# Loading and using the k-v-gate columns later in the first projection block, with six warming products in place of nine

## The chip, the cores and the metric

The kernel runs on one core of one Trainium2 chip. Time is device time in microseconds of one launch. The core has TensorE (PE, with its weight loads PEld), VectorE (DVE), ScalarE (ACT), GpSimd (POOL) and SyncE (SP); here SP issues all transfers of the kernel, and DMA engines carry them out.

## The reference

Two layers on the same tokens x (2048 x 640), mixed by a gate. The first is a Fourier mixing, real part of a transform over the hidden and the sequence axis, written as products with cosine and sine matrices. The second is attention of 32 heads of 20 with one shared key and value:

```
g = sigmoid((x * gate_w).sum(-1, keepdims=True))
a = Cr @ (x @ Wr.T) - Ci @ (x @ Wi.T)
q = heads(x @ wq);  k = x @ wk;  v = x @ wv
b = merge(softmax(q k^T / sqrt(20)) v) @ wo
out = g * a + (1 - g) * b
```

## The kernel before

Every fp32 operand of a product is kept as two parts: a high part rounded by ACT into the fp32r type, and a low part, the rest, computed by DVE. A product of two operands is then three products of parts: high by high, high by low, low by high (mm3, lines 122 to 124). In the names, wqh and wql are the parts of q's weights, xh and xl those of the transposed tokens, qh and ql those of q.

**The first stage**, where the change is, computes q, k, v and the gate's logits. The tokens are cut into four blocks of 512 (n = 0 to 3) and the hidden axis into five chunks of 128 (c = 0 to 4). q has five output groups of 128 rows (m = 0 to 4). k, v and the gate's column of weights stand side by side as 41 columns in one input, wkvg; its tile kvg is split into high columns 0 to 40 and low columns 64 to 104 of the tile kvgs. kv_mm (line 395) sends two products per chunk: one of xh with all 105 columns, one of xl with the high 41. In the last chunk their order is reversed.

Block 0 goes chunk by chunk, since the weights arrive chunk by chunk: load_x1 and move issue the loads (SP), split_x1 and split make the parts (ACT the high one, line 378 and 117; DVE the low one, line 379 and 118), then follow the chunk's k-v products and fifteen q products into six open PSUM banks. Blocks 1 to 3 go group by group.

Before the first data come, PE multiplies the identity by itself (line 106). These are the warming products; each is recorded as two pieces.

When a block's k-v sum is done, kv_out (line 402) evicts it: kvl (ACT, 408), kvT (DVE, 409), kh (ACT, 410), kl (DVE, 411), and six copies of kh and kl into the tile ks, which holds the keys for the score products. q_out (line 386) does the same for a q group: qh (ACT, 390), ql (DVE, 391), and two stores to the DRAM tensors qh_d and ql_d. load_qs0 (line 156) reads a first head pair back from there into the tile qs. The score products a (line 251), which search for the largest score of each query, are strewn among the q products of blocks 1 to 3, four at a time.

**Order.** PE, ACT, DVE and POOL execute in the order in which the program is written; so does SP's queue, except that loads are moved ahead to where their buffer is free. qh and ql have three buffers each, so the fourth qh of a block waits until the store of the first is done. Banks are taken by turns: line 350 for block 0, line 468 for the others, with four banks F1, V, S0 and F0. In block 1 the k-v sum takes F1, the transposed k-v of block 0 takes V, q groups 0 and 1 take S0 and F0, and q group 2 takes F1 again, once kv_out has emptied it.

The later stages are the Fourier products, attention and the output projection, interlaced on PE by hand-written orders. The change doesn't touch them.

## Time and profile before

| what | value |
|---|---|
| median of 3 runs | 1725.58 us (1724.9 to 1726.78) |
| profiled execution: span | 1723.7 us |
| profiled execution: time outside the span | not recorded; the median is 1.9 us above the span |
| PE busy | 1706.9 us, 99% of the span |
| DVE, ACT, POOL busy | 1379.9, 1251.9, 1103.8 us |
| granted TensorE clock, mean | 0.999 |
| block 0's first k-v product, block 1's first | at 5.95 and 26.47 us |

A row of the timeline gives the start and the duration in us, the engine, the line, the operation with what it writes and reads, and in brackets how long the engine had been idle before and what ended that. Starts of consecutive products are closer together than one product's duration, since PE overlaps them. A row SPq is SP issuing a transfer, not the transfer.

### The profile page before, as it was taken

The numbers are of one execution on the slowest core, as the hardware profiler recorded it, in microseconds if no ns is written. First come the engines' busy times: TensorE is split into PE (matmuls) and PEld (weight loads), VectorE is DVE, ScalarE is ACT, GpSimd is POOL, SyncE is SP. The second block draws the span as 40 slices with busy tenths as digits, with TensorE's granted clock in tenths as the row PEclk, the third lists the DMA queues.
The fourth block names the chain that finished last, engine by engine and source line by source line (L and its number), as shares of the span: only waits on it lengthen the run. The fifth ranks groups of instructions, "written<-read, shape, count | busy, mean of one in ns | idle before, by whom it ended". The sixth has DMA issues, their size and how long they took to land.

```text
span 1723.7 us, 43339 instructions
## 1 busy us (share of the span) xinstructions
PE 1706.9 (99%) x16754; PEld 1235.3 (72%) x16754; DVE 1379.9 (80%) x2294; ACT 1251.9 (73%) x2547; POOL 1103.8 (64%) x923
## 2 busy tenths in 40 slices
PE   9999999999999999999999999999999999999997
PEld 6686677777777777777777777777777777777665
DVE  4788888888888888888888888888888888888823
ACT  4247788888777677777777777777777767678896
POOL 0154556333356658758777888888887765547786
PEclk9999999999999999999999999999999999999999
DMA  8651223222275556546666666655555533143332
GB/s 251 190 157 58 72 79 106 79 71 72 65 232 170 172 164 198 170 157 201 220 214 218 226 233 227 205 186 184 177 179 165 159 113 114 52 128 110 108 94 95
DMA packets 180346, 261.46 MB, mean 152 GB/s; under 512 B 35568, under 2 KB 134128, under 8 KB 180140
## 3 DMA queue, kind: packets, MB, share of 16 engines
q1 hardware_dynamic: 180140, 258.70, 47.4%
q8 instruction: 132, 2.16, 0.5%
q14 instruction: 74, 0.61, 0.1%
HBM read 184.42 MB, written 76.99 MB: 152 GB/s over the span
## 4 chain that ended last, share of the span: by engine, by line
PE 96%; DMA 1%; ACT 1%; DVE 1%; SPq 1%; issue 1%; POOL 0%; DVEq 0%; ACTq 0%
PE av L983 27%; PE y_p L791 21%; PE b L971 18%; PE a L251 15%; PE ab L791 7%; PE oo L791 3%; PE q L122 1%; PE q L124 1%; PE q L123 1%; SPq L114 1%; ACT pt L979 1%; DMA qh_d<-qh 1%; PE kv L400 0%; DMA wraw<-in_wq_dram 0%; DVE pt L1028 0%
## 5 line engine op out<-in xcount | busy, mean ns | idle before, releaser
L258 DVE TENSOR_REDUCE mx<-a 128x1 f32<-128x512 f32 x2048 | 1304.4, 686 | 243.7 <-PE a L251 206.0
L979 ACT ACTIVATE pt<-b 128x512 f32<-128x512 f32 x2048 | 1058.5, 624 | 342.7 <-PE a L251 279.2
L971 PE MATMUL b<-qs,ks 62*128 62x512 f32 x2048 | 756.9, 408 | 2.2 <-ACT pt L979 1.4
L251 PE MATMUL a<-ks,qs 60*128 60x512 f32 x2048 | 704.2, 407 | 3.6 <-DMA qs<-ql_d 2.3
L791 PE MATMUL y_p<-tb,ch 64*128 64x320 f32 x3584 | 618.7, 307 | 0.0
L791 PEld LDWEIGHTS y_p<-tb,ch 64*128 64x128 f32 x3584 | 504.5, 186 | 2.9
L983 PE MATMUL av<-pt,vsb 128*32 128x512 f32 x4096 | 484.9, 597 | 0.0
L971 PEld LDWEIGHTS b<-qs,ks 62*128 62x128 f32 x2048 | 346.1, 184 | 186.4 <-DVE mx L258 124.2
L791 PE MATMUL y_p<-tb,cl 64*128 64x320 f32 x1792 | 455.5, 306 | 0.0
L251 PEld LDWEIGHTS a<-ks,qs 60*128 60x128 f32 x2048 | 345.2, 185 | 18.0 <-issue 4.7
L791 PEld LDWEIGHTS y_p<-tb,cl 64*128 64x128 f32 x1792 | 297.2, 185 | 2.8
L983 PEld LDWEIGHTS av<-pt,vsb 128*32 128x32 f32 x4096 | 111.4, 109 | 239.5 <-issue 229.6
L551 POOL TENSOR_TENSOR cl<-craw,ch 128x1024 fp32r<-128x1024 f32 x112 | 268.3, 2395 | 9.0
L833 POOL TENSOR_TENSOR yt<-yt,yu 128x320 f32<-128x320 f32 x86 | 75.8, 881 | 292.6 <-ACT yu L828 242.5
L833 POOL TENSOR_TENSOR abt<-abt,abu 128x320 f32<-128x320 f32 x64 | 55.7, 871 | 196.0 <-ACT abu L828 183.4
L545 POOL TENSOR_TENSOR craw<-craw 128x1024 f32<-128x1024 f32 x64 | 153.3, 2396 | 0.0
L550 POOL CAST ch<-craw 128x1024 fp32r<-128x1024 f32 x112 | 116.3, 1038 | 6.3 <-PE ab L791 2.2
L791 PE MATMUL oo<-wo,osp 64*128 64x320 f32 x816 | 91.6, 306 | 0.0
L791 PEld LDWEIGHTS oo<-wo,osp 64*128 64x128 f32 x816 | 86.7, 185 | 1.6
L577 POOL TENSOR_TENSOR tb<-braw,tb 128x320 fp32r<-128x320 f32 x80 | 69.7, 877 | 0.0
L791 PE MATMUL ab<-wbh,xh 64*128 64x320 f32 x256 | 59.4, 307 | 0.0
L791 PE MATMUL ab<-wbh,xl 64*128 64x320 f32 x256 | 59.3, 305 | 0.0
(138 smaller groups left out, 1604.0 us busy)
## 6 DMA issues: line engine op xcount, KB each, us to landing
craw<-in_cre_dram SPq DMA_DIRECT2D x80, 512.0 KB
craw<-in_cim_dram SPq DMA_DIRECT2D x64, 512.0 KB
s_d<-craw SPq DMA_DIRECT2D x32, 512.0 KB
craw<-s_d SPq DMA_DIRECT2D x32, 512.0 KB
braw<-b_d SPq DMA_DIRECT2D x80, 160.0 KB
xraw<-in_xT_dram SPq DMA_DIRECT2D x32, 320.0 KB
b_d<-abt SPq DMA_DIRECT2D x64, 160.0 KB
t_d<-braw SPq DMA_DIRECT2D x64, 160.0 KB
```

The source lines that it names most:

```text
L114: nc.sync.dma_start(words(dst), words(src))
L251: nc.tensor.matmul(ps, qs[v][b : b + 60, qb * P : (qb + 1) * P], ks[b : b + 60, c * ROW : (c + 1) * ROW], start=True, stop=True,)
L258: nc.vector.tensor_reduce(mx[v][:, hh, qb, c : c + 1], ps, axis=AX.X, op=ALU.max)
L545: nc.gpsimd.tensor_tensor(x, raw[0], x, op=how)
L550: nc.gpsimd.tensor_copy(h, x)
L551: nc.gpsimd.tensor_tensor(l, x, h.bitcast(F32), op=ALU.subtract)
L577: nc.gpsimd.tensor_tensor(t[:, 1], raw, t[:, 0].bitcast(F32), op=ALU.subtract)
L791: nc.tensor.matmul(ps, w, x, start=start, stop=stop)
L833: nc.gpsimd.tensor_tensor(t0, t0, t1, op=ALU.add)
L971: nc.tensor.matmul(ps, ks[b : b + 62, kc * P : (kc + 1) * P], qs[NPAIR * (qc // 2) + p][b : b + 62, (qc % 2) * ROW : (qc % 2 + 1) * ROW], ...
L979: nc.scalar.activation(t, ps, AF.Exp, scale=SCALE)
L983: nc.tensor.matmul(ps[32 * g : 32 * g + 32, :], vsb[:, kc, :], t, start=first, stop=last)
```

## The change

Four things are changed, all in the first stage.

- The load of kvg is issued behind the second chunk of q's weights, not ahead of the first, and it is split into kvgs after the second chunk's splits.
- Block 0's k-v products of a chunk are sent one chunk later: those of chunk c - 1 go behind the first two q groups of chunk c. The last chunk's go behind its third q group.
- The first chunk's q products go by terms: five high by high, five with xl, five with wql, each over the five groups.
- Six warming products are sent in place of nine.

```
--- before.py
+++ after.py
@@ -102,7 +102,7 @@
     omg = const.tile([P, NT], F32, name="omg")
 
     warm = bank("S4", "warm")
-    for _ in range(9):
+    for _ in range(6):
         nc.tensor.matmul(warm[:, :P], ident, ident, start=True, stop=True)
 
     nc.scalar.activation(gate, ident[:, :NT], AF.Exp)
@@ -437,7 +437,6 @@
             nc.vector.tensor_scalar(omg, gate, -1.0, 1.0, op0=ALU.mult, op1=ALU.add)
 
         load_x1(0, 0)
-        move(kvg, wkvg.rearrange("(c p) n -> p c n", p=P))
         pkv = rot("kv_0")
         pq = [rot(f"q_0_{m}") for m in range(KC)]
         for c in range(KC):
@@ -445,16 +444,27 @@
                 load_x1(0, c)
             raw = raw_tile([P, D], "wraw") if c in (2, 3) else w1.tile([P, D], F32, name="wraw", bufs=2)
             move(raw, wq_v[:, c])
-            if c == 0:
+            if c == 1:
+                move(kvg, wkvg.rearrange("(c p) n -> p c n", p=P))
+            split_x1(0, c)
+            split(raw, wqh[:, c], wql[:, c])
+            if c == 1:
                 nc.vector.tensor_copy(kvgs[:, :, :41], kvg)
                 nc.vector.tensor_tensor(
                     kvgs[:, :, 64:105], kvg, kvgs[:, :, :41].bitcast(F32), op=ALU.subtract
                 )
-            split_x1(0, c)
-            split(raw, wqh[:, c], wql[:, c])
-            kv_mm(pkv, 0, c)
+            if c == 0:
+                xh, xl = xsp[0]
+                for k, (w, x) in enumerate(((wqh, xh), (wqh, xl), (wql, xh))):
+                    for m in range(KC):
+                        nc.tensor.matmul(pq[m], w[:, 0, m * P : (m + 1) * P], x[:, 0], start=(k == 0), stop=False)
+                continue
             for m in range(KC):
                 q_mm(pq[m], 0, m, c)
+                if m == 1:
+                    kv_mm(pkv, 0, c - 1)
+                elif m == 2 and c == KC - 1:
+                    kv_mm(pkv, 0, c)
         for c in range(KC):
             load_x1(1, c)
         for c in range(KC):
```

In the changed kernel the lines from 438 on lie up to ten lines further down; the first chunk's q products are line 460 there, and the k-v-gate split is lines 452 and 453.

## The prediction

> **What bounds the kernel now.** I read the page first, then the waits of PE, then the timeline of the first 55 us, then the chain there. From the page, the span, PE's row and the chain that ended last:

> ```profile
> span 1723.7 us, 43339 instructions
> ...
> PE 1706.9 (99%) x16754; PEld 1235.3 (72%) x16754; DVE 1379.9 (80%) x2294; ACT 1251.9 (73%) x2547; POOL 1103.8 (64%) x923
> ...
> PE 96%; DMA 1%; ACT 1%; DVE 1%; SPq 1%; issue 1%; POOL 0%; DVEq 0%; ACTq 0%
> ```

> PE has work for 99% of the span, and the change neither removes nor adds a real product (only three warming ones go). So all that can move the time is when PE begins, at which clock, and how long it waits. The longest waits of PE over the whole run (total us, times, longest us):

> ```profile
> PE a L251 <- DMA qs<-ql_d: 2.3, 3, 1.0
> PE b L971 <- ACT pt L979: 1.4, 2, 0.7
> PE warm L106 <- POOL ident masks.py:199: 1.3, 1, 1.3
> PE o L122 <- DVE acc L774: 1.3, 1, 1.3
> PE a L251 <- DVE mx L258: 1.3, 1, 1.3
> PE q L122 <- DVE kvT L409: 0.9, 1, 0.9
> PE kv L400 <- DVE kvgs L450: 0.7, 1, 0.7
> ```

> The first, sixth and seventh row lie in the first 54 us, where the change is. The others come after that, or before the change, and follow PE's own pace. The beginning, from the timeline (start, us, engine, line):

> ```profile
> 1.17 0.42 SPq L114 DMA_DIRECT2D kvg<-in_wkvg_dram  x1
> 1.34 3.88 PE L106 MATMUL warm<-ident 128*128 128x128 f32 x18 [1.34 <-POOL ident masks.py:199]
> 1.63 0.52 SPq L114 DMA_DIRECT2D wraw<-in_wq_dram  x1
> 4.30 0.63 ACT L378 ACTIVATE xh<-xr 128x512 fp32r<-128x512 f32 x1 [2.08 <-DMA xr<-in_xT_dram]
> 5.03 0.37 DVE L449 CAST kvgs<-kvg 128x205 fp32r<-128x205 f32 x1 [5.03 <-DMA kvg<-in_wkvg_dram]
> 5.82 0.74 ACT L117 ACTIVATE wqh<-wraw 128x640 fp32r<-128x640 f32 x1 [0.89 <-DMA wraw<-in_wq_dram]
> 5.95 0.45 PE L400 MATMUL kv<-xh,kvgs 128*105 128x512 f32 x1 [0.73 <-DVE kvgs L450]
> 6.59 0.82 DVE L118 TENSOR_TENSOR wql<-wraw,wqh 128x640 fp32r<-128x640 f32 x1 [0.19 <-ACT wqh L117]
> 7.47 0.50 PE L124 MATMUL q<-xh,wql 128*128 128x512 f32 x1
> 7.81 0.39 PE L122 MATMUL q<-xh,wqh 128*128 128x512 f32 x1
> 8.89 0.83 DVE L118 TENSOR_TENSOR wql<-wraw,wqh 128x640 fp32r<-128x640 f32 x1 [0.18 <-ACT wqh L117]
> ```

> Two k-v products start at 5.95, one waits, two q products follow, and PE stands until wql is there (6.59 + 0.82 = 7.41). From 7.81 on it runs without a gap. The other end of this block, and what hangs on its k-v sum:

> ```profile
> 22.74 0.39 PE L400 MATMUL kv<-xh,kvgs 128*105 128x512 f32 x1
> 23.16 0.59 ACT L408 ACTIVATE kvl<-kv 41x512 f32<-41x512 f32 x1 [4.97 <-PE kv L400]
> 25.20 0.90 SPq L114 DMA_DIRECT2D ks<-kh  x1
> 26.47 0.40 PE L400 MATMUL kv<-xh,kvgs 128*105 128x512 f32 x1
> 30.06 0.42 SPq L114 DMA_DIRECT2D qh_d<-qh  x1
> 34.86 0.60 ACT L390 ACTIVATE qh<-q 128x512 fp32r<-128x512 f32 x1 [1.60 <-DMA qh_d<-qh]
> 36.55 0.67 DVE L409 TENSOR_TENSOR kvT<-kv,kvl 41x512 f32<-41x512 f32 x1
> 37.37 0.47 PE L122 MATMUL q<-xh,wqh 128*128 128x512 f32 x1 [0.87 <-DVE kvT L409]
> 42.09 1.19 PE L251 MATMUL a<-ks,qs 60*128 60x512 f32 x4 [0.98 <-DMA qs<-ql_d]
> 51.92 0.46 PE L251 MATMUL a<-ks,qs 60*128 60x512 f32 x1 [0.58 <-DMA qs<-ql_d]
> 53.11 0.70 PE L251 MATMUL a<-ks,qs 60*128 60x512 f32 x3 [0.73 <-DMA qs<-ql_d]
> ```

> The reader should see one chain here. The last k-v product of the block (22.74) ends it for ACT (23.16). kvl, kvT and kh follow, and then SP, which had stood idle, issues the first ks copy at 25.20. SP is now the narrow place: six ks copies, ten q stores behind them, six qs loads behind those, all in order on one queue. ACT's fifth qh waits for a store to free its buffer (34.86), kvl and kvT of the next block queue behind it, and PE waits at 37.37 for the bank that this kvT empties. The score products at 42.09, 51.92 and 53.11 wait for qs loads on the same queue. The chain view has the store itself, which competes with nothing but this chain:

> ```profile
> 31.05 3.71 DMA qh_d<-qh
> ```

> After 53.11 PE waits for nothing of SP's. So where PE stands at 53.11 is set by the moment at which the block's k-v sum is ready, with no play between, and not by the moment at which PE begins.

> **The change, part by part.** SP's queue at the start, of before and then of now (xr0 is the tokens' chunk, wraw the chunk of q's weights, kvg the k-v-gate columns):

> ```order
> L114 DMA xr0_144<-in_xT_dram 128x512
> L114 DMA kvg_137<-in_wkvg_dram 128x5x41
> L114 DMA wraw_153<-in_wq_dram 128x640
> L114 DMA xr0_180<-in_xT_dram 128x512
> L114 DMA wraw_182<-in_wq_dram 128x640
> ```

> ```order
> L114 DMA xr0_141<-in_xT_dram 128x512
> L114 DMA wraw_149<-in_wq_dram 128x640
> L114 DMA xr0_172<-in_xT_dram 128x512
> L114 DMA wraw_174<-in_wq_dram 128x640
> L114 DMA kvg_134<-in_wkvg_dram 128x5x41
> ```

> Four loads move up one place and kvg goes behind them. The first wraw is issued 1.63 - 1.17 = 0.46 us sooner, and kvg's bytes no longer go ahead of it: it landed 5.82 - 5.03 = 0.79 after kvg. I take 0.6, between these, so it lands at 5.22. ACT is free then (4.30 + 0.63 = 4.93), wqh is ready at 5.22 + 0.74 = 5.96, and PE starts 0.06 later as it did after wql (7.41, 7.47): first q product at **6.02**. Bounds: 5.73 when ACT never waits for the load, 6.62 when the load gains nothing.

> With five high products first, then five with xl, then five with wql, nothing waits in that chunk: xl is ready by 4.93 + 0.69 + a little, five products before its use, and wql at 5.96 + 0.03 + 0.82 = 6.81, ten before its use. The spacing of products comes from before: 80 products from 7.81 to 26.47 are 0.2333 us each; the first of a stretch takes 0.34 (7.47 to 7.81). Product 15, the first of chunk 1, starts at 6.02 + 0.34 + 14 x 0.2333 = 9.63, its first use of wql at 10.1; that wql was done at 8.89 + 0.83 = 9.72 even by before's loads. The two kvgs operations (0.37 each) go behind it on DVE, done by 10.5, and their first product is number 21, at 11.0. Queued behind them is chunk 2's xl and wql (1.5 us), used at 13.6: covered. Were the cover gone, each would cost its 0.74.

> PE's end of the block and the next block's first product, before (of the 15 q products behind the k-v pair only nine are shown) and now:

> ```order
> L124 MATMUL q_4_152<-xh,wql 128x512
> L400 MATMUL kv_147<-xl,kvgs 41x512
> L400 MATMUL kv_147<-xh,kvgs 105x512
> L122 MATMUL q_0_148<-xh,wqh 128x512
> L123 MATMUL q_0_148<-xl,wqh 128x512
> L124 MATMUL q_0_148<-xh,wql 128x512
> L122 MATMUL q_1_149<-xh,wqh 128x512
> L123 MATMUL q_1_149<-xl,wqh 128x512
> L124 MATMUL q_1_149<-xh,wql 128x512
> L122 MATMUL q_2_150<-xh,wqh 128x512
> L123 MATMUL q_2_150<-xl,wqh 128x512
> L124 MATMUL q_2_150<-xh,wql 128x512
> ```

> ```order
> L122 MATMUL q_2_146<-xh,wqh 128x512
> L123 MATMUL q_2_146<-xl,wqh 128x512
> L124 MATMUL q_2_146<-xh,wql 128x512
> L400 MATMUL kv_143<-xl,kvgs 41x512
> L400 MATMUL kv_143<-xh,kvgs 105x512
> L122 MATMUL q_3_147<-xh,wqh 128x512
> L123 MATMUL q_3_147<-xl,wqh 128x512
> L124 MATMUL q_3_147<-xh,wql 128x512
> L122 MATMUL q_4_148<-xh,wqh 128x512
> L123 MATMUL q_4_148<-xl,wqh 128x512
> L124 MATMUL q_4_148<-xh,wql 128x512
> L400 MATMUL kv_357<-xh,kvgs 105x512
> ```

> The last k-v product had fifteen products behind it and now has six: it was number 70 of the block's 85 and is number 79. It starts at 6.02 + 0.34 + 77 x 0.2333 = 24.33, where it started at 22.74: **1.6 us later**. The block itself ends sooner: 6.02 + 0.34 + 84 x 0.2333 = 25.96 against 26.47, **0.5 us sooner**. By the chain above the first number reaches PE whole, at 37.37 (now 38.95), and the second is spent waiting there: PE arrives earlier and waits some 3 us instead of 0.87. The later waits of 0.98, 0.58 and 0.73 stay as they are, since both sides moved by 1.6. In between, the evictions of q run 1.6 later as well, and PE needs the first of their banks only at 28.7, when ql0 is out at about 28.0.

> The three warming products: 18 pieces took 3.88, so twelve take 2.6 and end at 3.9. PE was idle from 5.22 anyway, so no time is won. What they may cost is the clock. All pieces of the warming, least, median and longest ns, and the last weight loads:

> ```profile
> L106 PEld LDWEIGHTS warm<-ident x18: 192/333/338, 1.3 to 4.8; 128*128 128x128 f32 x18
> 4.83 0.19 PEld L106 LDWEIGHTS warm<-ident 128*128 128x128 f32 x1
> ```

> The load at 4.83 is the first at 0.19, the pace of the rest of the run (L971: 184 ns); the median is 333. So PE came to full pace some 3.4 us after it began, although the granted clock of the windows says 1.00 throughout. [...] What is not shown is whether 2.6 busy of 3.4 us are enough. Bounds: nothing, or q products at half pace for 3.4 us or twice that. I take nothing, at even odds, because the runs of before differ by 1.9 us (1724.9 to 1726.78), about one such start, so their median may hold part of that price already. The idle stretch of 2.1 us between warming and first product is no danger once the clock is up:

> ```profile
> 1717.82 0.31 PE L124 MATMUL o_late<-wl,osp 128*128 128x320 f32 x1
> 1721.00:1723.70 2.70, 0.00 (x0) 0.00 (x0) 0.00 (x0) 0.00 (x0) 0.00 (x0) 0.62 0.46 180
> ```

> At the end PE stopped at 1718.1, and a mean clock of 0.62 over the last 2.7 us means half clock from about 1721.6: 3.5 us of idling were needed.

> Sum: 1723.7 + 1.6 = 1725.3 us of span. The profiled execution shows no time beside its span; the median of the runs is 1.9 above it, taken as what lies around it. So **1727.2 us**, 0.09% above 1725.58. The load's bounds make it +1.3 to +2.2.

> **Rivals.** About 0.2%, 3.45 us, is what a measurement of this kernel can tell from no change.

> *Cold start, short.* The first q products run at half pace until PE has again worked 3.4 us. By the weight loads (333 to 184) a product then takes 0.42 instead of 0.233; eight fit into 3.4 us, each 0.19 late: 1.5. The k-v sum is then 3.1 later: 1728.7. For it speaks that 2.6 us is less than 3.4, against it that no row shows so short a warming fail. Chance 0.22.

> *Cold start, long: slower.* If busy time is counted in fixed stretches of 3.4 us, those that are partly idle give nothing, and half pace lasts up to 6.8 us: 16 products, 3.0. More than ten slow products, or 4.2 us at half pace, carry it past 3.45 in all; I take 13 products, 2.5, so 1729.7, at most 1730.2. Chance 0.2.

> *The k-v chain has play.* If the 1.6 were absorbed (SP's queue catching up between 30 and 41, its stores running shorter), only PE's own 0.5 would show: 1725.1. Against it: SP issues without a pause from 25.20 to 33.9, and each later step waits for a store that began in this chain. Chance 0.07.

> That the change doesn't do what it says is excluded by the rows above. For a gain above 3.45 I see no mechanism, since all PE waits before 54 us together are about 4 and the chain gets later; 0.03 for what I overlook.

> **How the numbers follow.** Forecast 0.48, short cold start 0.22, long one 0.2, play 0.07, unforeseen gain 0.03. The measurement's half width adds about 0.7 to each. Slower by over 0.2%: most of the long case (0.17) and a third of the short one (0.07), 0.24. Faster 0.03. Within 0.2%: 0.73. The range runs from the play case, 1725.1, to the upper part of the long case, 1729.8, and leaves out about a tenth on either side.

> **What would show it.** In the profile after: the first q product near 6.0 with no wait of PE up to 26.0; the block's last k-v product near 24.3 and the first ks copy near 26.8; PE's wait of about 3 us before the third q group of the next block, at about 39; the score products at 43.7 and 54.7. Spacing of 0.42 in the first q products would show the cold start, and its length which one. The forecast is wrong if the ks copies start as late as I say and the score products do not, or if the first wraw does not land sooner.

## The result, and the profile after

The changed kernel takes 1731.0 us, median of 15 runs (1726.79 to 1732.84); the kernel before, 1725.94, median of 15 (1724.62 to 1728.61). The ratio is 1.0023, with a 95% interval of 1.0016 to 1.003: slower, by 2.8 to 5.2 us; the medians themselves lie 5.1 apart. The forecast was 1727.2, its range ended at 1729.8. The profiled execution took 1729.54, its span is 1727.8, 4.1 above that of before.

The timeline of after, the rows that answer to those shown of before (L460 are the first chunk's q products by terms):

```profile
1.34 2.93 PE L106 MATMUL warm<-ident 128*128 128x128 f32 x12 [1.34 <-POOL ident masks.py:199]
4.75 0.63 ACT L378 ACTIVATE xh<-xr 128x512 fp32r<-128x512 f32 x1 [2.52 <-DMA xr<-in_xT_dram]
5.55 0.74 ACT L117 ACTIVATE wqh<-wraw 128x640 fp32r<-128x640 f32 x1 [0.18 <-DMA wraw<-in_wq_dram]
6.34 1.43 PE L460 MATMUL q<-xh,wqh 128*128 128x512 f32 x5 [2.07 <-ACT wqh L117]
24.64 0.39 PE L400 MATMUL kv<-xh,kvgs 128*105 128x512 f32 x1
25.07 0.60 ACT L408 ACTIVATE kvl<-kv 41x512 f32<-41x512 f32 x1 [7.31 <-PE kv L400]
26.27 0.40 PE L400 MATMUL kv<-xh,kvgs 128*105 128x512 f32 x1
27.11 0.90 SPq L114 DMA_DIRECT2D ks<-kh  x1
39.31 0.77 PE L122 MATMUL q<-xh,wqh 128*128 128x512 f32 x1 [3.02 <-DVE kvT L409]
39.88 0.63 PE L123 MATMUL q<-xl,wqh 128*128 128x512 f32 x1
40.30 0.63 PE L124 MATMUL q<-xh,wql 128*128 128x512 f32 x1
44.41 0.98 PE L251 MATMUL a<-ks,qs 60*128 60x512 f32 x4
54.02 0.47 PE L251 MATMUL a<-ks,qs 60*128 60x512 f32 x1 [0.59 <-DMA qs<-ql_d]
55.20 0.71 PE L251 MATMUL a<-ks,qs 60*128 60x512 f32 x3 [0.71 <-DMA qs<-ql_d]
```

The chain is there as forecast. The k-v sum's last product starts at 24.64 (22.74 before), the ks copies at 27.11 (25.20), and PE, which is 0.2 us ahead of before at the block's end (26.27 against 26.47), waits 3.02 at the third q group. The first five q products take 1.43 together, 0.25 apart, near the 0.2333 of before. But from 39.31 on q products start 0.42 to 0.57 apart, and that is new. The windows of after, cut at the moments at which the granted clock changes (columns: PE busy, then PEld, DVE, ACT, POOL, the clock, DMA):

```profile
32.24:35.65 3.41, 3.41 (x16) 2.75 (x15) 0.00 (x0) 0.60 (x1) 0.00 (x0) 1.00 0.89 263
35.65:39.07 3.42, 0.65 (x3) 0.19 (x1) 1.95 (x4) 1.32 (x3) 0.00 (x0) 1.00 1.08 308
39.07:42.48 3.41, 3.17 (x8) 2.52 (x9) 2.58 (x5) 3.25 (x6) 0.00 (x0) 0.50 0.95 211
42.48:45.89 3.41, 3.41 (x16) 2.26 (x14) 1.98 (x4) 1.13 (x3) 0.00 (x0) 1.00 0.30 96
49.31:52.72 3.41, 3.41 (x17) 2.52 (x14) 0.48 (x1) 1.12 (x2) 0.00 (x0) 1.00 0.90 275
52.72:56.13 3.41, 2.11 (x9) 1.00 (x8) 3.41 (x7) 0.60 (x1) 0.00 (x0) 1.00 0.66 225
56.13:59.55 3.42, 3.42 (x9) 1.93 (x8) 2.78 (x5) 0.00 (x0) 0.00 (x0) 0.50 1.13 236
59.55:62.96 3.41, 3.41 (x18) 2.52 (x17) 1.16 (x3) 1.82 (x4) 0.00 (x0) 1.00 0.90 273
```

Twice a stretch of 3.41 us with a poorly used PE is followed by a stretch of 3.41 at half clock, in which 8 or 9 products run in place of 16 to 18. The first is the one with the long wait. The second follows the two shorter waits for qs, 0.59 and 0.71, that before had too, and kept its clock. In before, these and the two earlier waits were spread over four stretches (the place of their borders is taken from the fall at its end, near 1721.6):

```profile
35.45:38.86 3.41, 2.54 (x12) 1.77 (x11) 2.29 (x5) 2.31 (x6) 0.00 (x0) 1.00 1.05 297
38.86:42.28 3.42, 2.44 (x11) 1.67 (x9) 3.21 (x6) 2.79 (x6) 0.00 (x0) 1.00 0.58 139
49.10:52.52 3.42, 2.70 (x11) 1.65 (x9) 2.37 (x4) 0.78 (x2) 0.00 (x0) 1.00 0.48 154
52.52:55.93 3.41, 2.82 (x13) 1.72 (x13) 3.41 (x7) 0.00 (x0) 0.00 (x0) 1.00 1.07 320
```

How far PE is behind before, read at three marks of the timeline: at the third q group 39.31 - 37.37 = 1.94; at the score products 55.20 - 53.11 = 2.09; at the transposes of block 2:

```profile
59.89 0.44 PE L421 MATMUL kvt<-ident,kvT 41*128 41x41 f32 x4
```

Before had them at 56.22, so 3.67. The first stretch at half clock costs next to nothing, since PE, being late, no longer waits the 0.98 for qs at 44.41. The second costs 3.67 - 2.09 = 1.6 in full, since nothing is waited for behind it. So at 60 us, 2.1 us are the k-v sum and 1.6 the clock. That isn't the whole way to the 4.1 of the span. PE's last product ends only 3.01 later than in before (1721.13 against 1718.13), so 0.66 is won back on the way:

```profile
1720.82 0.31 PE L124 MATMUL o_late<-wl,osp 128*128 128x320 f32 x1
```

And from there to the end of the span after takes 6.62 us and before 5.53. These 1.1 us lie behind PE's work; why is not explained, and it may be one source of the spread.

### The profile page after: what moved, and what is told of

It is laid out like the page before. It is cut to its first block, busy times and chain, and to the rows that moved or that the text cites. A ratio compares the mean times of both kernels' runs of the same rounds, so it can differ in the third digit from the quotient of the medians.

```text
span 1727.8 us, 43324 instructions
## 1 busy us (share of the span) xinstructions
PE 1707.7 (99%) x16748; PEld 1236.2 (72%) x16748; DVE 1380.1 (80%) x2294; ACT 1251.7 (72%) x2547; POOL 1105.8 (64%) x923
## 4 chain that ended last, share of the span: by engine, by line
PE 96%; DVE 1%; ACT 1%; DMA 1%; issue 0%; SPq 0%; POOL 0%; DVEq 0%; ACTq 0%
PE av L993 27%; PE y_p L801 21%; PE b L981 18%; PE a L251 15%; PE ab L801 7%; PE oo L801 3%; PE q L122 1%; PE q L123 1%; PE q L124 1%; PE kv L400 1%; ACT pt L989 0%; DMA ql_d<-ql 0%; SPq L114 0%; DMA wraw<-in_wq_dram 0%; PE q L460 0%
## 5 line engine op out<-in xcount | busy, mean ns | idle before, releaser
L258 DVE TENSOR_REDUCE mx<-a 128x1 f32<-128x512 f32 x2048 | 1304.6, 686 | 242.7 <-PE a L251 195.9
L251 PE MATMUL a<-ks,qs 60*128 60x512 f32 x2048 | 703.5, 407 | 2.6 <-DMA qs<-ql_d 1.3
L251 PEld LDWEIGHTS a<-ks,qs 60*128 60x128 f32 x2048 | 345.0, 185 | 16.4 <-DVE mx L258 3.5
```

The source lines that it names most:

```text
L251: nc.tensor.matmul(ps, qs[v][b : b + 60, qb * P : (qb + 1) * P], ks[b : b + 60, c * ROW : (c + 1) * ROW], start=True, stop=True,)
L258: nc.vector.tensor_reduce(mx[v][:, hh, qb, c : c + 1], ps, axis=AX.X, op=ALU.max)
```

## The experiments

Each time is a median against the median of before on the same chip. The recorded expectations weigh three theories. W: the late k-v sum makes PE wait, and the clock falls to half after the wait. C: most executions start cold, that is, with PE at half pace. S: the clock is decided in fixed stretches of 3.41 us whose place differs from execution to execution, so six warming products fill one well enough only in some executions.

**The changed kernel again.**

> The changed kernel once more, beside the next three on one chip. Both theories below expect 4 to 5.5 us above before, as it was.

Measured: 1730.83 (9 runs) against 1726.33, ratio 1.0025 (1.0016 to 1.0035), 4.5 above before, as expected. Its profiled execution has a span of 1729.3 and shows what the first one did not, the cold start, and then the same two falls at another place:

```profile
6.38 2.50 PE L460 MATMUL q<-xh,wqh 128*128 128x512 f32 x5 [2.11 <-ACT wqh L117]
```

```profile
37.79:41.20 3.41, 0.43 (x3) 0.08 (x1) 1.87 (x4) 1.48 (x4) 0.00 (x0) 1.00 1.08 311
41.20:44.62 3.42, 3.42 (x8) 2.68 (x9) 2.92 (x5) 3.11 (x6) 0.00 (x0) 0.50 0.92 211
54.86:58.27 3.41, 2.27 (x10) 1.14 (x9) 3.41 (x7) 0.60 (x1) 0.00 (x0) 1.00 0.83 257
58.27:61.68 3.41, 3.41 (x12) 1.74 (x10) 2.23 (x4) 0.00 (x0) 0.00 (x0) 0.50 1.11 209
```

The first five products take 2.50 in place of 1.43. At the third q group this execution is 1.84 behind the other one (41.15 against 39.31): that is the price of the cold start. At the transposes of block 2, at 61.24, 1.35 of it are left. In both executions the two falls are 17.07 us apart, five stretches of 3.41, but they begin at 39.07 and 41.20. So in these two executions the clock fell and rose on a raster of 3.41 us, which lay 2.13 later against the program in the second.

**Nine warming products in the changed kernel, and the k-v pairs ahead of the last chunk.** One edit of the changed kernel each:

```
-    for _ in range(6):
+    for _ in range(9):
```

> The changed kernel with nine warming products again, all else as changed. Theory W (the wait): the late k-v sum makes PE wait 3.0 us at the third q group of block 1, the clock falls to half for about 3.4 us after that wait (and once more after the two waits of 0.6 and 0.7), and the warming has no part in it: time as the changed kernel, 0.2 to 0.3% above before, granted clock below 1 near 40 us again. Theory C (cold start in most runs, the profiled one being an exception): 1.5 to 3 us less than the changed kernel, so 0.1 to 0.15% above before.

```
+            if c == KC - 1:
+                kv_mm(pkv, 0, c - 1)
+                kv_mm(pkv, 0, c)
             for m in range(KC):
                 q_mm(pq[m], 0, m, c)
-                if m == 1:
+                if m == 1 and c < KC - 1:
                     kv_mm(pkv, 0, c - 1)
-                elif m == 2 and c == KC - 1:
-                    kv_mm(pkv, 0, c)
```

> The changed kernel, but in the last chunk both k-v pairs go ahead of its q products and not behind the second and third group. Theory W: the k-v sum is ready 9 products (2.1 us) sooner, the ks copies begin near 25, PE's wait at the third q group of block 1 is 1 us or a little more, the clock isn't lowered there, and the time is that of before, -0.5 to +0.5 us. Theory C: unchanged, 0.2 to 0.3% above before. A theory that the late k-v load or the order by terms costs the time expects the same 0.2 to 0.3%.

Measured: nine products 1728.65 against 1726.05, ratio 1.0013 (1.0004 to 1.0022). This lies between what the two theories expected: the warming seems to have a part, and it isn't all. Its profile has no cold start (the first five products take 1.43), but the long wait (2.98) and, as theory W expected, a fall of the clock at 40.39. K-v pairs ahead: 1727.82, ratio 1.0007 (0.9998 to 1.0016), so by its median 1.8 above before and not at its time. Its profile shows that the chain is healed and the start cold:

```profile
6.50 2.50 PE L460 MATMUL q<-xh,wqh 128*128 128x512 f32 x5 [2.24 <-ACT wqh L117]
39.04 0.47 PE L122 MATMUL q<-xh,wqh 128*128 128x512 f32 x1 [0.90 <-DVE kvT L409]
```

The wait is 0.90 as before, the clock doesn't fall, and in this execution all that is left came in at the start. Neither theory alone holds. Both losses are seen in profiles; by its time alone the second isn't shown, since its interval just reaches no change.

**Both undone together.** The changed kernel with both edits above:

> The changed kernel with nine warming products and, in the last chunk, both k-v pairs ahead of its q products: the loads, the order by terms and the other k-v products stay as changed. By theories W and S together, which put the whole loss into the late k-v sum and the six products, nothing of it is left: -0.6 to +0.3 us against before. If the late k-v load or the order by terms costs something, 0.5 us or more above before.

Measured: 1725.38 against 1726.33, ratio 0.9995 (0.9986 to 1.0004): 1.0 below by the medians, a little more than expected, and no difference by the interval. In its profile the block-2 transposes stand at 55.84, 0.38 ahead of before: about the half microsecond that the start was to bring. So neither the moved k-v load nor the order by terms shows a cost. With the three kernels above, this makes a square, in us above before:

| | six warming products | nine |
|---|---|---|
| last k-v pairs behind the q groups | +4.5 | +2.6 |
| ahead of them | +1.8 | -1.0 |

By these medians the late k-v sum costs 2.7 to 3.6, the three missing products 1.9 to 2.7. Each diagonal of the square was taken on a chip of its own, against before on that chip, and the interval of each entry reaches about 1.6 us to either side, so the sizes are rough.

**Each part in the kernel before.** The last k-v pair behind the third q group, alone:

```
-            kv_mm(pkv, 0, c)
+            if c < KC - 1:
+                kv_mm(pkv, 0, c)
             for m in range(KC):
                 q_mm(pq[m], 0, m, c)
+                if m == 2 and c == KC - 1:
+                    kv_mm(pkv, 0, c)
```

> The kernel before with one edit: the last chunk's k-v pair goes behind its third q group. Loads, warming and order of the first chunk are those of before. Theory W: the k-v sum is ready 9 products (2.1 us) later, PE waits about 3.0 us at the third q group of block 1 and the clock falls after it: 2.1 us and 1.4 for each stretch at half clock, so 3.5 to 5 us above before, 0.2 to 0.3%. Theory C and every theory that puts the loss into loads or warming: the time of before.

Measured: 1728.8 against 1726.05, ratio 1.0014 (1.0005 to 1.0023), so 2.8 above before, less than expected. In its profile PE waits 2.99 at the third q group, and the clock stays at 1.00, though two stretches there are less busy than one that made it fall in after (2.11):

```profile
34.56:37.97 3.41, 1.89 (x9) 1.18 (x7) 0.72 (x2) 1.61 (x4) 0.00 (x0) 1.00 1.09 284
37.97:41.38 3.41, 1.95 (x9) 1.62 (x9) 2.71 (x6) 2.34 (x5) 0.00 (x0) 1.00 1.04 272
41.38:44.80 3.42, 2.40 (x11) 1.49 (x10) 3.19 (x6) 2.36 (x5) 0.00 (x0) 1.00 0.51 140
```

By these windows the 3 us of waiting straddled the border at 37.97 and were shared between two stretches. Its transposes are at 58.17, 1.95 behind before: the chain's price without a fall of the clock.

Six warming products in the kernel before, alone:

> The kernel before with six warming products in place of nine, nothing else. Theory S (the clock goes by fixed stretches of 3.41 us, whose place differs from run to run; six products fill one stretch well enough only in about a third of the runs): in the other runs the first products go at half pace for 1 to 5 us, 0.5 to 2.5 us lost, so a median of 1 to 2 us above before. Theory W alone (only the late k-v sum and the clock after its wait): the time of before.

Measured: 1727.61 against 1726.33, ratio 1.0008 (0.9999 to 1.0016), 1.3 by the medians, where 1 to 2 were expected. The interval just reaches no change. The profiled execution shows two falls, though nothing of the k-v sum is moved here:

```profile
4.56:7.98 3.42, 1.86 (x6) 1.07 (x7) 2.46 (x5) 2.05 (x4) 0.35 (x1) 1.00 1.01 334
7.98:11.39 3.41, 3.41 (x9) 2.64 (x9) 2.73 (x5) 2.59 (x5) 0.00 (x0) 0.50 1.03 389
42.11:45.52 3.41, 2.15 (x9) 1.04 (x8) 3.06 (x5) 1.13 (x3) 0.00 (x0) 1.00 0.32 100
45.52:48.94 3.42, 3.42 (x10) 2.64 (x9) 1.92 (x4) 0.00 (x0) 0.00 (x0) 0.50 0.37 108
```

The q products at 6.74 and 6.97 start 0.23 apart, so here the six products had sufficed. Before its first real product PE had stood idle for 1.69 us, most of it in the stretch ahead of the first fall; from 8.07 on the q products start 0.43 apart. The second fall follows a stretch in which PE was idle for 1.26 (3.41 - 2.15).

**Filling the wait.** The changed kernel, with products of the identity where PE would wait:

```
             for m in range(KC):
+                if (n, m) == (1, 2):
+                    fill = bank("S1", "fill")
+                    for _ in range(12):
+                        nc.tensor.matmul(fill[:, :P], ident, ident, start=True, stop=True)
```

> The changed kernel with twelve products of the identity by itself (2.6 us at full pace, into a bank that is free) ahead of the third q group of block 1, where PE would wait. The k-v sum is as late as in the changed kernel. It tells the wait from the clock: by theory W the third q group starts at 39.3 as in the changed kernel, but the clock stays at 1.00 there, so 8 products are 0.19 us faster each: 1.5 us less than the changed kernel, up to 3 if the second stretch at half clock goes too. If the low clock were only a symptom, the time would be that of the changed kernel.

Measured: 1729.1 against 1726.05, ratio 1.0014 (1.0005 to 1.0022), 3.1 above before, 1.4 to 2.0 less than the changed kernel, though on another chip. In its profile the clock stays at 1.00 at the third q group, where PE waits 0.29; but the execution began cold (2.50 for the first five products), and the clock fell at 47.98, after a wait for qs of 1.06. The same with nine warming products:

> The changed kernel with nine warming products and with twelve products of the identity ahead of the third q group of block 1, so both ways to half pace are mostly shut and only the late k-v sum is left. Theories W and S: the prediction's own term alone, 1.6 to 2.2 us above before. If the wait costs little once the clock is held, 0.5 us or less above before; if it costs more than its length, over 3 us.

Measured: 1729.39 against 1726.27, ratio 1.0016 (1.0007 to 1.0025). A miss: with 3.1 it is no better than nine products without the filling (2.6). Its profiled execution, the fastest of its eleven runs at 1726.62, shows one reason. The third q group waits only 0.30, but the wait for qs, which the slow stretch had swallowed, is back:

```profile
44.24 1.18 PE L251 MATMUL a<-ks,qs 60*128 60x512 f32 x4 [1.15 <-DMA qs<-ql_d]
```

and the clock falls behind that one. In this execution the filling held the clock at the third q group and handed the wait on. So the times of the two filled kernels don't settle what the clock costs: the one is less than the changed kernel, the other no less than its own unfilled one.

That kernel once more, for one other execution:

> The kernel with nine warming products and the filled wait once more, for one other execution's profile, since its 11 runs lay between 1726.6 and 1732.9 and the profiled one was the fastest of them. If stretches at half clock make this spread, an execution 2 to 3 us slower shows two or more of them ahead of 60 us, each with about 8 products of 0.43 us, and the filling itself at half pace where one falls on it. If there are none, the spread comes from somewhere else and stays open.

Measured: 1728.14 in this execution, beside one of before of 1725.93. Up to 60 us the clock doesn't fall at all, and the block-2 transposes are at 58.44, 2.2 behind before. So the chain's 2 us are confirmed without a fall of the clock in them; the spread up to 1732.9 isn't explained by this execution.

**The other direction.** If the k-v sum sets PE's place at 54 us, an earlier one must gain. In chunk 3, the last token chunk is split ahead of its turn and the k-v products are sent at its head, in the changed kernel with nine and with eleven warming products, and in the kernel before. In the changed kernel these are the products of chunks 2 to 4, in the kernel before those of 3 and 4. The edit of the changed kernel, without the number of warming products:

```
-            if c:
+            if c and c < KC - 1:
                 load_x1(0, c)
...
-            split_x1(0, c)
+            if c < KC - 1:
+                split_x1(0, c)
             split(raw, wqh[:, c], wql[:, c])
+            if c == KC - 2:
+                load_x1(0, c + 1)
+                split_x1(0, c + 1)
...
+            if c == KC - 2:
+                for k in range(c - 1, KC):
+                    kv_mm(pkv, 0, k)
             for m in range(KC):
                 q_mm(pq[m], 0, m, c)
-                if m == 1:
+                if m == 1 and c < KC - 2:
                     kv_mm(pkv, 0, c - 1)
-                elif m == 2 and c == KC - 1:
-                    kv_mm(pkv, 0, c)
```

> The changed kernel with nine warming products and the k-v products of chunks 2, 3 and 4 all at the head of chunk 3, for which the last token chunk is split ahead of its turn; loads as changed. The k-v sum is ready near 19 in place of 23.2, and the ks copies begin behind the last token loads, near 21.5 in place of 25.2. Theory W: PE's waits of 0.9, 1.0, 0.6 and 0.7 us between 36 and 54 go, and with them every cause for the clock to fall there: 2 to 3.5 us below before. If the k-v sum does not set PE's place at 54 us, the time of before.

> The kernel before with the k-v products of chunks 3 and 4 both at the head of chunk 3, for which the last token chunk is split ahead of its turn; loads, warming and the first chunk as before. Theory W: the k-v sum some 2 to 4 us sooner, PE's waits between 36 and 54 us mostly gone: 1.5 to 3 us below before. If the gain of the early kernel came from the loads and the order by terms: the time of before.

> The early k-v kernel with eleven warming products, so that PE works nearly without a break from 1.3 to its first q product. Theory S: a full stretch is filled in more runs, and no later than at 8.2; 0 to 0.8 us less than with nine (0.15% below before), with less spread over the runs. If nine were enough in every run: the same time, or 0.2 us more.

Measured: with nine 1723.57 against 1726.33, ratio 0.9985 (0.9976 to 0.9994); in the kernel before 1723.99 against 1726.27, 0.9988 (0.9979 to 0.9997); with eleven **1722.23** against 1726.27, ratio 0.9976 (0.9967 to 0.9985). The first two came as theory W had it, and the third beats both kernels; over nine it gains more than the 0 to 0.8 expected, and its runs spread more (1721.4 to 1725.34), not less. In the first, PE's waits up to 120 us are these alone:

```profile
PE warm L106 <- POOL ident masks.py:199: 1.3, 1, 1.3
PE a L251 <- DVE mx L258: 1.3, 1, 1.3
PE q L464 <- ACT wqh L117: 0.8, 1, 0.8
PE a L251 <- DMA qs<-ql_d: 0.5, 1, 0.5
```

although that execution began cold:

```profile
6.33 2.50 PE L464 MATMUL q<-xh,wqh 128*128 128x512 f32 x5 [0.78 <-ACT wqh L117]
```

Nine products are thus not enough in every execution. With eleven PE works on until the first q product, and the first five are faster than in a cold start:

```profile
1.34 5.06 PE L106 MATMUL warm<-ident 128*128 128x128 f32 x22 [1.34 <-POOL ident masks.py:199]
6.47 1.65 PE L464 MATMUL q<-xh,wqh 128*128 128x512 f32 x5
```

Its gain over nine, some 1.3 us by the medians, was taken on two chips. This profiled execution is the slowest of the eleven, at 1725.34, and shows that an early k-v sum doesn't exclude a fall. One comes at 51.33, after waits of 0.66 and 0.65:

```profile
47.92:51.33 3.41, 2.10 (x9) 0.98 (x8) 3.41 (x7) 0.60 (x1) 0.00 (x0) 1.00 0.63 213
51.33:54.75 3.42, 3.42 (x9) 1.82 (x10) 2.92 (x5) 0.00 (x0) 0.00 (x0) 0.50 1.13 243
```

## Why the prediction was wrong

**The sum, and the two terms that failed.** The forecast was 1.6 us for the late k-v sum, nothing for the three missing warming products, and nothing for the clock after the longer wait. By the square, the late sum cost 2.7 to 3.6 (2.8 alone in the kernel before), and the missing products 1.9 to 2.7 (1.3 alone there). So "I take nothing" for the warming is the term furthest off, and the k-v term lacks what the clock adds to it. The cold-start rivals stood on the 1.6 and ended at 1730.2; a price for the clock after the wait stood in none of them.

**The start: right.** The first q product was to come at 6.02, within 5.73 to 6.62; it came at 6.34. Wraw landed sooner, but by 0.27 and not by 0.6: its split starts at 5.55, before 5.82. The token chunk ahead of it landed later (4.75, before 4.30), but that isn't what held wqh up: ACT was done with the chunk at 5.38 and then idle for 0.18 until wraw came. In all profiles with the changed loads the chunk lands at 4.71 to 4.90, in those with the old ones at 4.30 to 4.51. Nothing waited behind the first product, as forecast.

**The k-v chain: right, a little too small.** 1.6 was forecast. In after the sum's last product starts 1.9 later, the 0.3 above the forecast being that of the start, and PE is 1.94 and 2.09 behind. With the old loads and the start of before, where the pair moves by nine products, 1.95 arrive. The 3 us of waiting, its place and what PE waits for came out as said, and the play rival is refuted: the ks copies start 1.9 later and everything behind them does.

**"The later waits of 0.98, 0.58 and 0.73 stay as they are": wrong for the first.** PE at half clock arrived after qs was there.

**"3.5 us of idling were needed": the step that failed in the k-v term.** The fall at the kernel's end, after a wholly idle time, shows that so much idling was enough, not that it was needed. I took it for the condition, and so gave the forecast 3 us wait no price beyond its length. A stretch with 0.65 us of work, and even one with 2.11 to 2.27, was enough. The second stretch at half clock cost 1.6 in after. By the same reading the idle time between warming and first product was "no danger once the clock is up"; in the kernel before with six products the clock was up and fell at 7.98, after a stretch in which PE was busy for 1.86 us.

**"I take nothing, at even odds": the step that failed in the warming term.** The cold start was foreseen as a rival, at 0.42 in all, and its sizes, 1.5 and 2.5, were good: the one that was traced in after's kernel cost 1.84 at the third q group. It is neither always there nor never; in after's own profile it is missing. The reason given for nothing, that the median of before may hold part of the price already, left out that six products can cost more than nine: by the square's medians they do, by 1.9 to 2.7. That the clock might go by fixed stretches of 3.4 us stood in the long rival as an assumption, which no row of before shows. I weighed it for the start alone, and not for the waits; in after, two stretches at half clock in the middle of the run are 3.41 long each and 17.07 apart.

**What stays open.** Busy time alone doesn't decide the fall: 1.89 and 1.95 of 3.41 in the late-pair kernel kept the clock, 2.11 and 2.27 in after lost it; the latter hold four score products of 60 rows in place of 128. That alone isn't the reason either: the stretch from 53.64 to 57.05 in the second execution of the filled kernel holds four of them, is busy for 2.19, and kept the clock. Nor does a trace show how many falls each untraced run had, so the medians' 4.5 to 5.1 are not split more finely than by the square.

## What to carry to other kernels

Follow a moved operation to the queue that it feeds, not to the engine that it runs on: in the late-pair kernel a place nine products later in a full PE stream cost 1.95 us by way of SP. A wait of PE can have two prices, its length and the clock after it: the wait of 3 us was followed by 3.41 us at half clock in both profiles of the changed kernel, and not in that of the late-pair kernel, where it was shared between two stretches. So one profile may show the second price or not. Where such starts and waits matter, look at more than one execution, and keep PE busy up to its first real product: the early k-v kernel took 1722.23 with eleven warming products and 1723.57 with nine.

## What the runs showed of the hardware

```profile
132.56:135.97 3.41, 2.74 (x16) 1.00 (x16) 1.51 (x3) 3.27 (x8) 1.31 (x3) 1.00 0.03 8
135.97:139.38 3.41, 3.41 (x20) 1.03 (x14) 0.03 (x1) 0.50 (x2) 3.25 (x5) 0.50 0.14 48
```

- The granted clock in the windows says 1.00 from the span's start, also where the first products start cold: in the early k-v kernel with nine warming products it says 1.00 from 6.85 to 10.27, where 9 products run, in place of the 16 of the next stretch. The cold start is read from the products (the first five take 1.43 or 2.50 us together), not from that column.
- The first token chunk landed 0.2 to 0.6 us later with the 320 KB of weights issued right behind it than with the 102.5 KB of kvg, in every profile. That the later load delays the earlier one may be the reason; it was not tried by itself.
